# The state's read of an attention and bilinear kernel on 64-row tiles, with its two halves summed after scaling

## The chip, the cores and the metric

The kernel runs on one core of a Trainium2 chip. The metric is the device time of one execution in microseconds (us), lower is better. The core has TensorE (PE in the rows; its weight loads are listed apart as PEld), VectorE (DVE), ScalarE (ACT), GpSimd (POOL) and SyncE (SP), which here only starts transfers. TensorE writes its results into PSUM, which the kernel takes in pairs of banks of 128 partitions by 512 fp32 columns; VectorE and ScalarE read them there and write into SBUF.

## The reference

Each of 8 batches with 8 heads has 512 tokens `x` and 32 states `state`, both 64 wide. Tokens read the states and states read the tokens; all the rows then pass a bilinear layer.

```python
scores = scale * x @ state.T           # per batch and head; a = softmax(scores)
xread = a @ state                      # 512 rows
scores2 = scale * state @ x.T          # a2 = softmax(scores2)
sread = a2 @ x                         # 32 rows: the state's read
rows = concat([xread, sread])          # heads side by side: 4608 x 512 in all
out = ((rows @ w1) * (rows @ w2)) @ w3 @ w_out
```

All inputs and the output are fp32.

## The kernel before

The two last weights are multiplied into one ahead of the batches (`f`, `m` and `k` steps), while `w1` and `w2` come in and are converted. Everything large is computed as a high and a low part: a value is rounded to fp32r (`high`, on ScalarE), the remainder is taken (`low`, on VectorE), and TensorE adds three products of the parts. The state's read and the scores are small and use plain fp32 products; TensorE runs each of these as two passes, so 32 products are 64 records in the trace.

The work is cut into some 1,300 named steps. No scheduler orders them: the tables OPENING, SCRIPTS and CLOSING list their names, and each engine runs its part of the steps in that order. In SCRIPTS, which is followed once for each of batches 2 to 7, `+` stands for the next batch and `*` for the one after it. A batch `b` takes these steps:

- `sP`: scores of states against tokens. 8 products (`per_head`, line 201), each 64 rows deep (one head) and 32 columns of the array wide: two heads times four column strips, hence eight tiles of 64*32, in two PSUM banks, one for each half of the rows. `sM`, `sN`, `sE`, `sA`, `sB` make softmax over tokens with the sum's reciprocal in `sum2`, `sT` to `sV` the softmax over states; `sW` and `sQ` turn the first and move it, so that tokens lie on the partitions (`a2`).
- `u0p` to `u3p`: states against `w1` and `w2`, four steps of 8 products in the same form as `sP` (line 201 too). `u..h` (ScalarE) and `u..l` (VectorE, line 174) split them and so free their banks.
- `rP`: the state's read, line 362. For each of 2 head halves (`kt`), 4 token tiles (`t`) and 4 head pairs (`j`) one product over 128 tokens: 32 columns of the array, 64 moving columns. The four head pairs lie on four column strips of the array (128*32), and the four token tiles are added up in one PSUM bank. `rS` multiplies by the reciprocal of the sum on VectorE (line 371), `rV` transposes (line 378), `rQ` moves 16 blocks into `sread`, which is used at the very end only.
- `a0` to `a7` (line 417): the bilinear factors, 12 products each; `c` copies one factor, `m` multiplies by the other.
- `P1` to `P7` (lines 220 and 225): one level of Strassen products with the fused weight; `v` steps (line 177 and copies) add them up, `d` steps store.

PSUM is handed out as four pairs of banks in rotation from batch 1's `a` steps on: a step on TensorE that starts a new pair takes the one that the fourth such step before it used, and so waits until VectorE and ScalarE have read that one. In the batches 3 to 7 the order on TensorE is `P4`, `u0p`, `rP`, `u1p`, `u2p`, `u3p`, `sP` (of the next batch; batch 7 has none to follow), `P6`, `P7`. So `u1p` takes the pair of `P2` and `P4`, which the last two `v5` sums free; `u3p` takes the pair of `u0p`, which `u0l` frees; `sP` takes the pair of `rP`, which `rS` frees.

Of the kernel before, what the change touches and what calls it, by code (L numbers as in the profile page):

```python
# [57 lines left out]
1:sh g2A 0:o1 g2C 1:sl g2B 1:t 1:u0l 0:d0 g2D 1:sW 0:z2 g30 g2h g2l g3A 1:sQ g31 g3C g3B 0:d1 0:o3 1:u1h 0:o2  # L58
g3D 1:u2h 0:d3 0:rQ 1:u1l 1:u2l g3h g3l 0:d2 paired 1:a0 1:c0 1:u3p 1:m0 1:u3h 2:sP 1:a1 1:rP 1:c1 2:sT 1:u3l
1:a4 2:sM 2:sR 2:sN 2:t 2:sS 1:m1 2:sE 2:sX 2:sC 1:B0d 1:a2 1:A0h 1:c4 1:a3 2:sD 2:sF 2:sG 1:rS 1:a5 1:B0h 1:m4  # L60
2:sV 1:c2 1:a6 1:A0l 1:B0l 2:sW 1:c5 1:c3 1:m2 2:sA 1:m3 1:c6 1:B1d 1:B1h 1:m5 1:A1h 1:a7 1:D0x 1:c7 1:m6 1:A1l
1:B1l 1:m7 1:D1x 1:P1 1:D0y 1:P2 1:E0h 2:sh 2:sl 1:C0h 1:v1a 1:F0h 1:v1b 1:C1h 1:C0l 1:C1l 1:D1y 1:rV 1:v2a
1:E0l 2:sQ 1:P3 1:D1z 3:x 1:G0h 1:F0l 1:F1h 1:E1h 1:v3a 1:F1l 1:v2b 1:P5 1:E1l 1:P4 1:D0z 1:v3b 1:G0l 1:rQ 2:rP
1:G1h 1:v5a 1:G1l 1:H0h 1:v5b 1:v5c 1:H1h 2:u0p 1:v5d 2:sB 1:H0l 2:u1p 2:u2p 2:rS 2:u0h 2:u0l 3:t 2:u1h 2:u2h
2:u1l 3:sP 2:u2l 3:sT 1:d5 2:u3p 2:u3h 3:sM 3:sN 1:P6 1:H1l 1:v6a 3:sE 2:rV 2:u3l 1:d3 1:P7 1:v6b 1:v6c 1:v7a
1:v7b 1:d6 1:d7 2:rQ
# [15 lines left out]
CLOSING = """
7:a0 7:a1 7:a3 7:c1 7:c0 7:m0 7:a2 7:c2 7:m1 7:a5 Rw00h 7:c3 7:m2 7:m3 7:c5 7:A0h 7:a4 7:c4 7:B0d 7:m4 7:m5 7:a6
7:A1h 7:B0h 7:B1d 7:B1h 7:B0l 7:B1l 7:c6 7:a7 7:C0h 7:c7 7:A0l 7:A1l 7:m7 7:m6 Rw01h 7:P1 Rw10h 7:v1a 7:E0h
7:C1h 7:P2 7:E1h 7:D0x 7:D0y 7:v2a 7:C0l 7:v1b 7:D1x 7:F0h 7:C1l 7:D1y 7:v2b 7:D1z 7:F0l 7:F1h R0 7:F1l 7:P3
7:G0h 7:E1l 7:P5 Rw11h 7:v3a 7:D0z 7:G1h 7:E0l 7:v3b 7:G0l 7:P4 7:v5a 7:H0h 7:v5b 7:G1l Rw00l 7:v5c 7:H0l Rw01l
7:v5d 7:P6 7:v6a Ra00 7:d3 Rw10l Ra01 7:H1h 7:v6b 7:v6c Rw20h 7:d5 Rc0 7:H1l Rm0 Rx0 Rw20l Rw11l Ra10 Rw21h
Rw30h 7:P7 Rw30l Ra11 7:d6 Rw31h Rd0 7:v7a Rw21l Ra20 Rw31l Rc1 Ra21 Ra30 Rw40h Rw41h Rc2 RA0h Rw40l Rm1 Rx1
Rw50h Ra31 7:v7b Rw51h Rw41l Rd1 Rw50l Ra40 Ra41 Rm2 RA1h Ra50 Rc3 Rw51l Rm3 Rw60h RA1l Ra51 Rx2 Rw61h Rc4 Rx3
Rw60l Ra60 Rm4 Rw70h Rw61l Rd2 Rd3 Rx4 7:d7 Rc5 RA0l Re0 RA2h Rm5 Rw70l R2P0 Rf0 Rx5 Ra61 Re1 Rg0 R1P0 Rf1 RA3h  # L90
Ra70 R2P1 Rc6 RA3l RF0h RA2l Rw71h RE1h Rm6 Rg1 R2P2 RE0h R2P3 Rv2 Rx6 Rw71l Re2 RE1l R1P1 Rf2 RF0l Rg2 Ra71
RE0l RE2h R1P2 R1P3 RE2l R6P0 Rc7 R4P0 Rm7 R4P1 R6P1 Rx7 R5P0 Re3 R4P2 Rv1 Rf3 R5P1 RE3h R6P2 R5P2 Rg3 RF2h RE3l
R5P3 RF1h RF2l RF3h R4P3 RF1l R6P3 RF3l Rv5 Rv4 R7P0 R7P1 Rv6 Rv8 R7P2 R7P3 R3P0 Rv7 R3P1 R3P2 Ro1 R3P3 Rv3 Ro0
"""


# [955 lines left out]
```

## Time and profile before

| | |
|---|---|
| Median of 3 runs | 480.27 us (480.11 to 480.42) |
| The profiled execution | 480.09 us |
| Its span, first to last instruction | 478.3 us |
| TensorE busy | 472.1 us (99%), 3226 records |
| VectorE busy | 415.0 us (87%), 642 instructions |
| ScalarE busy | 240.0 us (50%) |
| Granted TensorE clock, mean | 0.999 |
| One batch of the loop | 47.24 us |

The span is the profiled execution's, and the execution took 1.8 us more than it. A busy share says what an engine does over the whole; what limits a stretch is told by the waits and by the chain of waits, which goes back from the last instruction to whatever released it, or to the instruction before it on its engine.

### The profile page before, as it was taken

Reading aid. Unit: us, or ns where it says so; the run is one execution under the profiler, and the core shown is the slowest. Engines: PE = TensorE matmul, PEld = TensorE weight load, DVE = VectorE, ACT = ScalarE, POOL = GpSimd, SP = SyncE. Lnnn points to the kernel's source line nnn. Section 1 sums busy time; section 2 is a strip of 40 time slices with the busy share of each in tenths; the row PEclk is TensorE's granted clock in tenths of the full one; section 3 lists DMA queues with packets and bytes.
Section 4 is the critical chain, followed back from the end, with each engine's and each line's share of the span. In section 5 each row is a group of like instructions: output and inputs, shape, how many; then the busy total and the mean of one; then the engine's idle time right before and its main releaser. Section 6 shows DMA issues by size and latency. Waiting matters only on the chain.

```text
span 478.3 us, 8331 instructions
## 1 busy us (share of the span) xinstructions
PE 472.1 (99%) x3226; PEld 364.2 (76%) x3226; DVE 415.0 (87%) x642; ACT 240.0 (50%) x381; POOL 0.2 (0%) x4
## 2 busy tenths in 40 slices
PE   8999999999999999999999999999999999999996
...
DVE  5889998998999988997999799979997996399995
...
GB/s 339 428 423 391 240 165 98 88 112 103 14 121 110 136 105 69 38 121 134 25 43 126 129 31 44 122 126 29 50 124 27 32 37 72 2 0 45 23 24 44
DMA packets 56359, 52.45 MB, mean 110 GB/s; under 512 B 42752, under 2 KB 50944, under 8 KB 51712
## 3 DMA queue, kind: packets, MB, share of 16 engines
...
q8 instruction: 25, 0.41, 0.4%
...
## 4 chain that ended last, share of the span: by engine, by line
PE 92%; DMA 3%; ACT 2%; DVE 1%; issue 0%; SPq 0%; ACTq 0%
PE ps L417 37%; PE ps L220 19%; PE ps L225 10%; PE ps L201 8%; PE ps_o L773 5%; PE ps_o L559 5%; PE ps L847 3%; DMA x_d<-in_x_d_dram 2%; PE ps L362 2%; PE ps L849 2%; DMA raw<-in_w_k_dram 1%; PE ps L951 1%; ACT w_sb L671 1%; PE ps_o L951 1%; ACT ulps L684 1%; DVE w_sb L696 0%
## 5 line engine op out<-in xcount | busy, mean ns | idle before, releaser
L417 PE MATMUL ps<-at_lo,sw_hi 128*128 128x512 f32 x256 | 100.0, 391 | 0.0
L417 PE MATMUL ps<-at_hi,sw_hi 128*128 128x512 f32 x256 | 99.8, 390 | 0.0
L417 PE MATMUL ps<-at_hi,sw_lo 128*128 128x512 f32 x256 | 99.7, 390 | 0.0
L427 ACT COPY tmp<-ps 128x512 f32<-128x512 f32 x64 | 36.1, 586 | 70.6 <-PE ps L417 36.0
L177 DVE TENSOR_TENSOR tmp<-tmp,ps 128x512 f32<-128x512 f32 x81 | 54.6, 681 | 4.6 <-PE ps L225 2.9
L417 PEld LDWEIGHTS ps<-at_lo,sw_hi 128*128 128x128 f32 x256 | 48.1, 188 | 11.6 <-issue 1.7
L220 PE MATMUL ps<-t,g_hi 128*128 128x512 f32 x224 | 56.7, 395 | 0.0
L417 PEld LDWEIGHTS ps<-at_hi,sw_lo 128*128 128x128 f32 x256 | 48.0, 188 | 10.1
L417 PEld LDWEIGHTS ps<-at_hi,sw_hi 128*128 128x128 f32 x256 | 48.1, 188 | 9.8
L220 PEld LDWEIGHTS ps<-t,g_hi 128*128 128x128 f32 x224 | 40.1, 188 | 12.3 <-DVE sw_lo L174 4.3
L180 ACT CAST sw_hi<-ps 128x1024 fp32r<-128x1024 f32 (+1 forms) x34 | 31.4, 970 | 33.1 <-PE ps L201 33.1
L220 PE MATMUL ps<-wo,g_hi 128*128 128x512 f32 x168 | 42.4, 394 | 0.0
L174 DVE TENSOR_TENSOR sw_lo<-ps,sw_hi 128x1024 fp32r<-128x1024 f32 (+1 forms) x34 | 38.0, 1152 | 5.0 <-ACT sw_hi L180 4.6
L446 DVE TENSOR_TENSOR g_x<-tmp,ps 128x512 f32<-128x512 f32 x28 | 18.5, 676 | 22.5 <-ACT tmp L427 22.5
L220 PEld LDWEIGHTS ps<-wo,g_hi 128*128 128x128 f32 x168 | 30.7, 188 | 6.1
L225 PEld LDWEIGHTS ps<-t,g_lo 128*128 128x128 f32 x224 | 30.5, 190 | 2.3
L201 PE MATMUL ps<-w_sb,st 64*32 64x512 f32 (+1 forms) x544 | 31.4, 570 | 0.0
L225 PE MATMUL ps<-t,g_lo 128*128 128x256 f32 x224 | 31.1, 281 | 0.0
L174 DVE TENSOR_TENSOR g_lo<-g_x,g_hi 128x512 fp32r<-128x512 f32 (+2 forms) x50 | 31.1, 630 | 0.0
L180 ACT CAST g_hi<-g_x 128x512 fp32r<-128x512 f32 (+2 forms) x50 | 27.9, 579 | 4.2 <-DVE g_x L446 4.2
L180 ACT CAST g_hi<-raw 128x512 fp32r<-128x512 f32 x42 | 25.3, 620 | 9.4 <-DVE raw L174 6.2
L174 DVE TENSOR_TENSOR g_lo<-raw,g_hi 128x512 fp32r<-128x512 f32 x42 | 28.2, 682 | 0.0
...
## 6 DMA issues: line engine op xcount, KB each, us to landing
...
sread<-turned SPq DMA_DIRECT2D x128, 4.0 KB, 1.8
```

The lines of the kernel that those rows point to most:

```text
L174: nc.vector.tensor_tensor(out=out, in0=x, in1=y, op=ALU.subtract)
L177: nc.vector.tensor_tensor(out=out, in0=x, in1=y, op=ALU.add)
L180: nc.scalar.copy(out=hi, in_=src)
L201: nc.tensor.matmul(ps[j * NS:(j + 1) * NS, q], states[rows, j], moving(rows, j), start=True, stop=True)
L220: nc.tensor.matmul(ps[:, tt].rearrange("p (n d) -> p n d", n=2), g, w(k), start=(fresh and k == 0), stop=False, skip_group_check=True,)
L225: nc.tensor.matmul(ps[:, tt, :HO], g, w(k)[:, 0], start=False, stop=(k == QF - 1), skip_group_check=True)
L417: nc.tensor.matmul(ps[:, i], w[:, kt, c:c + P], a[:, kt], start=(k == 0), stop=(k == 3 * KT - 1))
L427: nc.scalar.copy(out=copies[ft], in_=sums[ft][:, 0])
L446: nc.vector.tensor_tensor(out=whole, in0=copies[ft], in1=sums[ft][:, 1], op=ALU.mult)
L559: nc.tensor.matmul(ps[:, :DO], g, wo[w][:, ft, :], start=(ft == 0 and k == 0), stop=(ft == FT - 1 and k == 2))
L773: nc.tensor.matmul(w34_ps[i][:, :DO], a, w, start=(len(started) == 1 and n == 0), stop=(len(started) == FT and n == len(terms) - 1),)
L847: nc.tensor.matmul(ps[:, i], wh[:, kt], sr[:, kt], start=(kt == 0), stop=False)
```

## The change

Each product of the state's read is cut in two along the tokens: tokens 0 to 63 of a tile on the upper 64 rows of the array, 64 to 127 on the lower 64. There are 64 products instead of 32, on eight tiles of 64*32, and the halves go into the two banks of the pair, each of which is added up over the four token tiles. `rS` scales both banks at once, 256 columns instead of 128. `rV` first adds the two halves, 128 columns within SBUF, and then transposes as before.

```diff
-            ps = two_banks()[:, 0, :KT * D].rearrange("p (k d) -> p k d", k=KT)
+            ps = two_banks()[:, :, :KT * D].rearrange("p i (k d) -> p i k d", k=KT)
             for kt in range(KT):
                 for t in range(NT):
                     for j in range(NP):
                         mine = slice(j * NS, (j + 1) * NS)
-                        nc.tensor.matmul(
-                            ps[mine, kt], s["a2"][:, kt, t * P + j * NS:t * P + (j + 1) * NS],
-                            s["tokens"][:, t, 2 * j + kt], start=(t == 0), stop=(t == NT - 1),
-                        )
+                        for i in range(2):
+                            rows = slice(i * D, (i + 1) * D)
+                            nc.tensor.matmul(
+                                ps[mine, i, kt], s["a2"][rows, kt, t * P + j * NS:t * P + (j + 1) * NS],
+                                s["tokens"][rows, t, 2 * j + kt], start=(t == 0), stop=(t == NT - 1),
+                            )
...
-            s["scaled"] = att.tile([P, KT, D], F32, name="scaled", bufs=1)
+            s["scaled"] = att.tile([P, 2, KT, D], F32, name="scaled", bufs=1)
             nc.vector.tensor_tensor(
-                out=s["scaled"], in0=s["read"], in1=s["sum2"].unsqueeze(2).broadcast_to([P, KT, D]), op=ALU.mult
+                out=s["scaled"], in0=s["read"], op=ALU.mult,
+                in1=s["sum2"].unsqueeze(1).unsqueeze(3).broadcast_to([P, 2, KT, D]),
             )
...
+            both = s["scaled"].rearrange("p i k d -> p i (k d)")
+            add(both[:, 0], both[:, 0], both[:, 1])
             s["turned"] = att.tile([P, KT, D], F32, name="turned")
-            nc.vector.transpose(
-                out=s["turned"].rearrange("p k d -> p (k d)"), in_=s["scaled"].rearrange("p k d -> p (k d)")
-            )
+            nc.vector.transpose(out=s["turned"].rearrange("p k d -> p (k d)"), in_=both[:, 0])
```

The three tables list the same step names in a new order, from batch 1's `sh` on; two lines show the manner.

```diff
-F1h +sl F1l D0z G0h P3 E0h v2b E0l P5 E1h E1l H0h D1z v3a G1h v5a P4 +u0p v3b G1l v5b H1h +rP G0l v5c d3 v5d
-+u0h *t +u1p +u2p +u1h +u2h +rS +u0l +u3p *sP H0l +u1l +u2l +u3h +u3l +rV *sM P6 v6a H1l P7 *sN *sT v6b v6c +rQ
...
+P5 v2a E1l E0l v3a v2b G0h D0z P4 v3b v5a +u0p D1z H0h v5b G0l v5c H1h v5d +rP +u1p G1h G1l +u0h +u1h +u0l +rS
+d3 +u1l +u2p +u2h +u3p +u3h H0l *sP P6 H1l +u2l *sM *sN v6a *t d5 +u3l P7 *sT +rV ?x v6b v6c *sR +rQ *sE v7a v7b
```

On TensorE most of the order stays. In each batch `a1` now comes ahead of `a0` and `a4` ahead of `a3`; batch 1 takes its `a` steps as 2, 3, 5, 4, 7, 6 instead of 4, 2, 3, 5, 6, 7; batch 2's read moves behind its `u0p`; and a few products of the closing change places with each other. At three places the order of the instructions before and after reads as follows. In such a row stand the line, the operation, what is written from what, the output's partitions and columns, and how many such instructions follow each other.

TensorE in batch 4, from the end of `P4` on (L220, L225) over `u0p`, `rP`, `u1p` to `u3p` and `sP` to `P6`; before:

```order
L225 MATMUL ps_2355<-t,g_lo 128x256 x8
L201 MATMUL ps_2471<-w_sb,st 32x512 x8
L362 MATMUL ps_2484<-x_s,e_2375 32x64 x32
L201 MATMUL ps_2527<-w_sb,st 32x512 x8
L201 MATMUL ps_2536<-w_sb,st 32x512 x8
L201 MATMUL ps_2554<-w_sb,st 32x512 x8
L201 MATMUL ps_2563<-x_d,st 32x512 x8
L220 MATMUL ps_2583<-t,g_hi 128x512 x8
```

And now:

```order
L225 MATMUL ps_2497<-t,g_lo 128x256 x8
L201 MATMUL ps_2597<-w_sb,st 32x512 x8
L364 MATMUL ps_2617<-x_s,e_2480 32x64 x64
L201 MATMUL ps_2682<-w_sb,st 32x512 x8
L201 MATMUL ps_2705<-w_sb,st 32x512 x8
L201 MATMUL ps_2717<-w_sb,st 32x512 x8
L201 MATMUL ps_2730<-x_d,st 32x512 x8
L220 MATMUL ps_2739<-t,g_hi 128x512 x8
```

The places are the same; the read is 64 products instead of 32.

VectorE at the same place, from the `v5` sums (L177) over the read's scaling (L371, now L373) and the subtractions `u0l` to `u3l` (`sw_lo`) to the transpose of the read (L378, now L383); `g_lo` are splits for the products `P6` and `P7`. Before:

```order
L177 TENSOR_TENSOR tmp<-tmp,ps_2355 128x512 x2
L371 TENSOR_TENSOR scaled<-ps_2484,sum_2137 128x128
L174 TENSOR_TENSOR sw_lo<-ps_2471,sw_hi 128x1024
L174 TENSOR_TENSOR g_lo<-raw,g_hi 128x512
L174 TENSOR_TENSOR sw_lo<-ps_2527,sw_hi 128x1024
L174 TENSOR_TENSOR sw_lo<-ps_2536,sw_hi 128x1024
L174 TENSOR_TENSOR sw_lo<-ps_2554,sw_hi 128x1024
L378 STREAM_TRANSPOSE turned<-scaled 128x128
```

And now:

```order
L177 TENSOR_TENSOR tmp<-tmp,ps_2497 128x512 x2
L174 TENSOR_TENSOR g_lo<-g_x,g_hi 128x512
L174 TENSOR_TENSOR sw_lo<-ps_2597,sw_hi 128x1024
L373 TENSOR_TENSOR scaled<-ps_2617,sum_2275 128x256
L174 TENSOR_TENSOR sw_lo<-ps_2682,sw_hi 128x1024
L174 TENSOR_TENSOR g_lo<-raw,g_hi 128x512 x2
L174 TENSOR_TENSOR sw_lo<-ps_2705,sw_hi 128x1024
L266 TENSOR_REDUCE m_2758<-ps_2730 128x2
L270 TENSOR_SCALAR m_2758<-m_2758 128x2
L177 TENSOR_TENSOR tmp<-tmp,ps_2739 128x512
L174 TENSOR_TENSOR sw_lo<-ps_2717,sw_hi 128x1024
L276 STREAM_TRANSPOSE work<-ps_2730 128x1024
```

The scaling has moved behind `u0l`, one split ahead of `u0l`, and the last two subtractions go later; the new sum and the transpose follow the last of these rows.

TensorE in batch 2, from the end of `P4` to `P6`; before:

```order
L225 MATMUL ps_1309<-t,g_lo 128x256 x8
L362 MATMUL ps_1453<-x_s,e_1351 32x64 x32
L201 MATMUL ps_1497<-w_sb,st 32x512 x8
L201 MATMUL ps_1509<-w_sb,st 32x512 x8
L201 MATMUL ps_1518<-w_sb,st 32x512 x8
L201 MATMUL ps_1542<-x_d,st 32x512 x8
L201 MATMUL ps_1556<-w_sb,st 32x512 x8
L220 MATMUL ps_1571<-t,g_hi 128x512 x8
```

And now:

```order
L225 MATMUL ps_1401<-t,g_lo 128x256 x8
L201 MATMUL ps_1530<-w_sb,st 32x512 x8
L364 MATMUL ps_1539<-x_s,e_1363 32x64 x64
L201 MATMUL ps_1608<-w_sb,st 32x512 x8
L201 MATMUL ps_1618<-w_sb,st 32x512 x8
L201 MATMUL ps_1629<-w_sb,st 32x512 x8
L201 MATMUL ps_1641<-x_d,st 32x512 x8
L220 MATMUL ps_1673<-t,g_hi 128x512 x8
```

The read has gone from the head of the run to its second place, as in the later batches.

## Rows read from the trace of the kernel before

**Rows 1.** The page's busy times, share of the span and instructions of each engine, and the slices of TensorE and VectorE: busy tenths in 40 equal slices of the span.

```profile
PE 472.1 (99%) x3226; PEld 364.2 (76%) x3226; DVE 415.0 (87%) x642; ACT 240.0 (50%) x381; POOL 0.2 (0%) x4
...
PE   8999999999999999999999999999999999999996
...
DVE  5889998998999988997999799979997996399995
```

**Rows 2.** TensorE's waits over the whole span, all that there are: who waited for whom, us in total, times, longest us.

```profile
PE ps_o L738 <- DVE w_sb L696: 1.2, 1, 1.2
PE ps_o L143 <- DVE work L140: 1.0, 1, 1.0
PE ps L201 <- DMA x_d<-in_x_d_dram: 0.2, 1, 0.2
```

**Rows 3.** The chain of waits in order of time, TensorE's pieces of line L201 that stand between others with no read of the state ahead of them (the last one has it ahead): start, us, what, records.

```profile
72.98 1.88 PE ps L201 x32
...
83.24 1.02 PE ps L201 x16
...
100.73 2.74 PE ps L201 x48
```

**Rows 4.** The same chain at the eight reads of the state (L362), batches 0 to 7, with the pieces of L201 beside them; for batch 2 from the chain of the stretch 153 to 160 us.

```profile
99.70 1.03 PE ps L362 x64
...
122.41 1.03 PE ps L362 x64
...
153.97 1.03 PE ps L362 x64
155.00 4.54 PE ps L201 x80
159.54 0.04 issue
...
201.23 1.02 PE ps L201 x16
202.25 1.05 PE ps L362 x64
203.30 3.59 PE ps L201 x64
...
248.48 1.02 PE ps L201 x16
249.50 1.03 PE ps L362 x64
250.53 3.59 PE ps L201 x64
...
390.19 1.02 PE ps L201 x16
391.21 1.03 PE ps L362 x64
392.24 2.73 PE ps L201 x48
```

**Rows 5.** The instructions of line L362 in batches 1 to 7: duration min/median/max in ns, first and last start, form (rows*columns of the array, then the moving operand).

```profile
L362 PEld LDWEIGHTS ps<-x_s,e x448: 106/110/110, 122.3 to 392.0; 128*32 128x32 f32 x150
L362 PE MATMUL ps<-x_s,e x448: 216/219/243, 122.3 to 392.0; 128*32 128x64 f32 x150
```

**Rows 6.** VectorE's groups of instructions by line and form: out<-in, count, busy us, mean ns of one, idle before and what ended it. A sum out of PSUM, the read's scaling, and a sum of 128 columns within SBUF.

```profile
L177 DVE TENSOR_TENSOR tmp<-tmp,ps 128x512 f32<-128x512 f32 x81 | 54.6, 681 | 4.6 <-PE ps L225 2.9 <-ACT tmp L859 0.3
...
L371 DVE TENSOR_TENSOR scaled<-ps,sum 128x128 f32<-128x128 f32 x8 | 2.3, 289 | 3.5 <-PE ps L362 3.5
...
L177 DVE TENSOR_TENSOR tmp<-g_x,tmp 128x128 f32<-128x128 f32 x4 | 1.1, 288 | 0.1
```

**Rows 7.** One batch of the loop, from one `u0p` to the next: the stretch and its length, then busy us (records) of PE, PEld, DVE, ACT and POOL, granted clock, DMA share, GB/s.

```profile
248.41:295.65 47.24, 47.24 (x353) 37.38 (x352) 42.25 (x63) 21.05 (x35) 0.00 (x0) 1.00 0.28 82
```

**Rows 8.** VectorE's timeline at batch 5's read: start, us, engine, line, operation, count, idle before it and what ended that.

```profile
295.98 1.40 DVE L177 TENSOR_TENSOR tmp<-tmp,ps 128x512 f32<-128x512 f32 x2
297.84 0.29 DVE L371 TENSOR_TENSOR scaled<-ps,sum 128x128 f32<-128x128 f32 x1 [0.47 <-PE ps L362]
298.05 1.21 DVE L174 TENSOR_TENSOR sw_lo<-ps,sw_hi 128x1024 fp32r<-128x1024 f32 x1
299.18 0.68 DVE L174 TENSOR_TENSOR g_lo<-raw,g_hi 128x512 fp32r<-128x512 f32 x1
```

**Rows 9.** TensorE's timeline at the same place.

```profile
295.65 1.09 PE L201 MATMUL ps<-w_sb,st 64*32 64x512 f32 x16
296.67 1.10 PE L362 MATMUL ps<-x_s,e 128*32 128x64 f32 x64
297.70 2.81 PE L201 MATMUL ps<-w_sb,st 64*32 64x512 f32 x48
300.30 1.06 PE L201 MATMUL ps<-x_d,st 64*32 64x512 f32 x16
301.30 0.50 PE L220 MATMUL ps<-t,g_hi 128*128 128x512 f32 x1
```

**Rows 10.** The page's DMA queues that carry instructions: packets, MB, share of 16 engines' span.

```profile
q8 instruction: 25, 0.41, 0.4%
```

**Rows 11.** The first tenth of a microsecond of batch 5's `u1p`, line L201 alone: the stretch and its length, busy us (records) of PE and of PEld, granted clock, DMA share, GB/s.

```profile
297.68:297.78 0.10, 0.08 (x8) 0.08 (x16) 1.00 0.00 0
```

More of the change, by code (lines that the diff above doesn't have):

```diff
@@ L57 @@
 0:l7 1:sF 0:e7 g1B 1:sA 0:rP g1D 1:u0p g1C 1:sB g1h 1:sG 0:rS 0:o0 1:u1p g1l 1:u2p g20 0:z3 1:sV 0:rV g21 1:u0h
[L58 to L66, printed above, removed]
+1:sh g2A 0:o1 g2C 1:sl g2B 1:t 1:sW 1:sQ 1:u0l 0:d0 g2D 0:z2 g30 g2h g2l g3A g31 g3C g3B 0:d1 0:o3 1:u1h 0:o2
+g3D 1:u2h 0:d3 0:rQ 1:u1l 1:u2l g3h g3l 0:d2 paired 1:a0 1:u3p 2:sP 1:c0 1:m0 2:sM 1:u3h 1:a1 1:c1 1:u3l 2:sT
+2:sN 3:x 1:rP 2:sR 2:sE 2:sS 2:sX 2:sA 1:rS 1:m1 1:B0d 1:a2 1:a3 1:a5 2:sC 1:c2 1:B0h 1:m2 2:sD 2:sF 1:c3 1:B0l
+2:sG 1:m3 1:c5 1:rV 1:a4 1:A0h 2:sV 1:c4 1:B1d 1:a7 2:sW 1:A0l 1:B1h 1:A1h 1:a6 1:c7 1:m4 1:m5 1:D0x 1:m7 1:B1l
+1:C0h 1:C0l 2:sB 1:c6 1:A1l 1:m6 1:D1x 1:D0y 2:t 2:sQ 1:P1 1:P2 1:v1a 1:C1h 1:F0h 1:v1b 1:C1l 1:E0h 1:P3 1:D1y
+1:E1h 1:G0h 1:D1z 1:E1l 1:F1h 1:D0z 1:F0l 1:F1l 1:P5 1:v3a 1:E0l 1:v2a 1:v3b 1:v2b 2:sh 2:sl 1:H0h 1:G0l 1:v5a
+1:v5b 1:P4 1:v5c 1:rQ 1:v5d 1:H0l 2:u0p 2:rP 1:G1h 2:u0h 2:u1p 2:u0l 2:u3p 2:rS 2:u2p 2:u1h 3:sP 2:u3h 2:u1l
+2:u2h 2:u3l 1:G1l 3:sT 3:sM 1:H1h 4:x 1:d3 2:u2l 3:sN 1:H1l 1:P6 1:v6a 1:v6b 2:rV 2:a1 3:sR 3:sE 1:v6c 1:P7 2:c1
+1:d5 2:a0 1:d6 1:v7a 1:v7b 2:c0 1:d7 3:t 2:a2 2:rQ
 """
@@ L70 @@
     None: """
-+sA a0 +sR a1 c0 c1 m0 m1 *x B0d +sS A0h A0l B0h B0l a2 +sX a3 +sC +sD +sF +sG c2 m2 c3 +sV a4 m3 c4 m4 B1d B1h
-A1h a5 c5 +sB a6 +sW m5 c6 B1l m6 C0h C0l A1l a7 D0x +sh c7 m7 P1 v1a D0y D1x F0h P2 v1b C1h D1y +sQ F0l C1l v2a
-F1h +sl F1l D0z G0h P3 E0h v2b E0l P5 E1h E1l H0h D1z v3a G1h v5a P4 +u0p v3b G1l v5b H1h +rP G0l v5c d3 v5d
-+u0h *t +u1p +u2p +u1h +u2h +rS +u0l +u3p *sP H0l +u1l +u2l +u3h +u3l +rV *sM P6 v6a H1l P7 *sN *sT v6b v6c +rQ
-d5 *sE d6 v7a v7b d7
++sS m0 m1 +sA A0h B0d A0l B0h +sX a4 a3 +sC +sD +sF +sG c3 c2 B0l +sB m2 m3 +sV a5 c4 B1d m4 c5 B1h A1h a6 m5
+D0x a7 c6 m6 c7 C0h +sW +sh A1l D0y C0l B1l m7 P1 +sQ P2 D1x F0h D1y v1a C1h v1b +sl E0h C1l E1h P3 F0l F1h F1l
+P5 v2a E1l E0l v3a v2b G0h D0z P4 v3b v5a +u0p D1z H0h v5b G0l v5c H1h v5d +rP +u1p G1h G1l +u0h +u1h +u0l +rS
+d3 +u1l +u2p +u2h +u3p +u3h H0l *sP P6 H1l +u2l *sM *sN v6a *t d5 +u3l P7 *sT +rV ?x v6b v6c *sR +rQ *sE v7a v7b
+d6 +a1 +a0 +a2 +c0 d7 +c1
 """,
@@ L82 @@
 CLOSING = """
[L83 to L92, printed above, removed]
@@ L93 @@
-R5P3 RF1h RF2l RF3h R4P3 RF1l R6P3 RF3l Rv5 Rv4 R7P0 R7P1 Rv6 Rv8 R7P2 R7P3 R3P0 Rv7 R3P1 R3P2 Ro1 R3P3 Rv3 Ro0
+7:m0 7:a3 7:c2 7:m1 7:a4 7:m2 7:B0d 7:a5 7:c3 7:c5 7:m3 7:c4 7:B0h 7:B0l 7:A1h Rw00h 7:A0h 7:a6 7:m4 7:m5 7:c6
+7:a7 7:B1d 7:D0x 7:A0l 7:C0h 7:m6 7:A1l 7:c7 7:m7 7:B1h 7:B1l 7:P1 7:E0h 7:C1h Rw01h 7:C0l 7:D0y 7:v1a 7:P2
+7:C1l 7:v1b 7:F0h 7:E1h 7:P3 7:D1x 7:D1y 7:E1l 7:F0l 7:D0z 7:F1h 7:v2a 7:E0l 7:F1l 7:v3a 7:G0h 7:v3b 7:v2b 7:D1z
+7:d3 Rw00l 7:P5 R0 7:v5a 7:P4 7:G0l 7:H0h 7:G1h 7:v5b 7:G1l 7:P6 7:H1h 7:v5c 7:v5d Ra00 7:H0l 7:v6a Rw10h Rw11h
```

7 lines of the change are left out of this document (added).

## The prediction

> **What bounds the kernel now.** I read the busy times first, then TensorE's waits, then the chain of waits, then the two neighbourhoods that the change touches. TensorE is busy for 472.1 of 478.3 us, with a 9 in 38 of the 40 slices, and VectorE for 87% [rows 1]. TensorE's own list of waits holds 2.4 us in all, and all of it comes before the pieces that the new order touches: the three names in it are the zeros of the warm-up, a weight conversion and the first load of x [rows 2]. So from about 35 us on the time is what TensorE's instructions take one behind the other. A change can gain only by making that sequence shorter, and it can lose by making TensorE wait. No order of the same instructions can win more than those 2.4 us, and the new order leaves that stretch alone; so I credit the reordering with no gain.
>
> The sequence is read best from the chain of waits, because its pieces run from start to start. A step of eight products on 64*32 tiles (line L201, 16 records, two passes for each fp32 product) takes 1.02 us when it stands alone, two in a row take 1.88, three 2.74 [rows 3], four 3.59 [rows 4]. So one more step of this form costs 0.86, and about 0.16 is paid once for each unbroken run, at its ends. Eight products lie on eight tiles (two halves of rows, four of columns), so a step is two passes deep: 0.43 us for 512 columns, 0.84 ns for a column. The state's read (L362) is 64 records of 64 columns on 128*32 tiles [rows 5]; on four tiles that is 16 passes deep, 16 x 64 x 0.84 ns = 0.86 us. The chain gives it 1.03 [rows 4]. The 0.17 beyond the passes is again the price of the ends. In six of the eight batches the read stands beside steps of the other form: first in such a run in batches 0 and 2, inside it in 3 to 7, so there the run of 64*32 steps is cut and its 0.16 is paid twice.
>
> **The read itself.** It becomes 128 records on 64*32 tiles. They lie on eight tiles instead of four, so they stay 16 passes deep: 0.86 us again, and no gain inside. What goes are the ends. I take 0.88 for a read in the middle of a run, 0.02 for the doubled starts. The floor is 0.86, since the same 64 columns go through each tile 16 times and the 64-row form has no faster column in any row; the upper end of this term is 1.03, if the read still pays its own ends. That the pairs may not run side by side at all is the first rival.
>
> Batches 3 to 6, from the step before the read to the end of the run [rows 4]: 1.02 + 1.05 + 3.59 = 5.66 once and 1.02 + 1.03 + 3.59 = 5.64 three times; after: 1.02 + 4 x 0.86 + 0.88 = 5.34. That is 0.32 + 3 x 0.30 = 1.22. Batch 7 has one step less: 1.02 + 1.03 + 2.73 = 4.78 against 4.48, 0.30. Batch 0: 1.03 [rows 4] + 2.74 [rows 3] = 3.77 against 1.02 + 2 x 0.86 + 0.88 = 3.62, 0.15. Batch 2 now takes 1.03 + 4.54 + 0.04 of issue = 5.61 [rows 4]; its five steps alone would be 4.46, so 0.12 of it is waiting for VectorE, which I leave in: 4.46 + 0.88 + 0.12 = 5.46, 0.15 (0.27 if the waiting goes). Batch 1's read stands between 128*128 products and stays alone: 0.88 + 0.16 = 1.04 against 1.03, a loss of 0.01. Sum: 1.22 + 0.30 + 0.15 + 0.15 - 0.01 = 1.81 us less.
>
> **VectorE's additions.** The scaling reads 256 columns instead of 128. From 289 ns for 128 columns and 681 for a 512-column sum out of PSUM [rows 6] a column costs 1.02 ns, so 0.13 more. The new sum over 128 columns is the form that takes 288 ns in the same list. That is 0.42 us a batch: 42.25 of 47.24 us [rows 7] becomes 42.67 of about 46.9. The cover is the 4 us that VectorE stays idle; without it each batch would be 0.42 longer, 3.4 in all. ScalarE, at half its time, gets nothing. The transpose and the copies behind it only have to land before the last rows are read.
>
> **Waits at the seam.** With the run shorter, TensorE asks earlier for two banks. The step after the read takes the bank that two sums (L177 x2) free at 295.98 + 1.40 = 297.38 [rows 8]; it started at 297.70 [rows 9]. It would now start 0.86 + 0.88 and some part of 0.16 behind 295.65, at 297.39 to 297.55. The third step after the read takes the bank of the step that stands ahead of the read, freed by the subtraction at 298.05 + 1.21 = 299.26; it started at 297.70 + 0.88 + 0.86 = 299.44. It would now ask at 299.11 to 299.27. In the new order this subtraction no longer stands behind the scaling, which had waited 0.47 us for the read; one split of 0.68 us goes ahead of it instead, so it runs about 297.90 to 299.11. A bank is passed on in about 0.04 (the issue piece in [rows 4]). Both margins shrink to between 0.12 and nothing: I take 0.02 a batch for six batches, 0.1, with ends of 0 and 0.15 a batch (0.9). The scaling itself now ends at about 299.5, ahead of the next scores, which take its bank at about 300.0. The first 128*128 product after the run takes the bank of the first step after the read, and the subtraction that frees this bank moves up by one split, so that margin grows. In the batches' other places the new order swaps neighbours (second product step before the first, fifth before the fourth). No row prices that; the nearest is the 0.12 of waiting in batch 2. I take 0, with ends of 0 and 0.5 over the kernel; below nothing is excluded by [rows 2].
>
> **Instructions fetched.** The queue with 25 packets and 0.41 MB [rows 10] carries, by its count, TensorE's 6,452 records: 258 to a packet, 0.4% x 16 x 478.3 / 25 = 1.2 us each. One read now is 256 records, a packet's worth, in 0.9 us. If a read begins just where a packet does, TensorE may wait for the next: 0 to 1.2 us in a batch, likely in none or one. I take 0 and keep 1.2 for the range.
>
> Sum: 1.81 - 0.1 = 1.7 less. The profiled execution took 480.09 us for its span of 478.3; that gives 478.4. Against the median of 480.27 it is 478.6. I forecast 478.5.
>
> **Rivals.** *The instructions come too slowly* (slower). One read issues 256 records (128 products' passes and as many weight loads) in the time of 128. The densest long stretch of the trace is the present read, 128 records in 1.03 us, 8.0 ns each. At that pace a read takes 2.06, less ends 1.9, which is 1.0 more in each of eight: 478.5 + 8 = 486.5. It decides from 0.88 + 1.7/8 = 1.09 us a read, 4.3 ns a record. For it: nothing in the trace has been faster for so long. Against it: the 1.03 is already explained by columns and ends, and at the head of a run 8 matmuls and 16 weight loads start within 0.08 us, 3.3 ns each [rows 11], on the very tiles that the read will use. The Trainium skill, "TensorE: Matmul & The Clock Gate", section "Wait — 56ns, not 53.3ns?", says that start-to-start never drops below about 25 ns however small a matmul is; by it 128 starts would be an estimated 3.2 us a read, over 17 us more in all. This trace does not agree: 64 starts in 1.03 us are 16 ns each.
>
> *The ends stay* (no effect). If a run is broken by any new operand and not by the tile's form, the read pays its ends as before: no gain, 480.2. Against it: the scores, from other tensors than the three steps ahead of them, join their run: the piece of 3.59 in [rows 4] holds them, 0.85 above three steps; in [rows 9] they follow without a gap.
>
> *The gain is waited away* (within 0.2%). At 0.15 a batch in six batches, 0.5 in swapped places and no other loss, 478.4 + 1.3 = 479.7.
>
> **How the numbers follow.** A difference of 0.2%, 0.96 us, is about what a measurement of this kernel can tell from none. The forecast, 477.8 to 479.3, has 0.62. Waited away has 0.12, ends stay 0.07, together the 0.19 of no change; slow supply, in full or in part (481.2 to 486.5), has 0.17; 0.02 lies below. So faster 0.64, same 0.19, slower 0.17. The range goes from 477.6 to 481.3 and leaves out the slow supply.
>
> **What would show it.** In the chain after, a run of the batches 3 to 6 with the read inside is one stretch of about 5.34 us, and the read adds 0.88 to it; a read near 1.9 is the first rival, 1.03 with 0.16 on either side the second. The third step after the read shows no idle time, or some hundredths behind the subtraction. The scaling takes 0.42 and the new sum 0.29. The period of a batch falls from 47.24 to about 46.95. I am wrong if TensorE's list of waits holds more than 1 us beyond the 2.4 of now.

## The result, and the profile after

The changed kernel takes 486.6 us (median of 4 runs, 486.52 to 487.71) against 480.25 (480.11 to 480.42) on the same chip: 1.0137 times as long, 95% interval 1.012 to 1.0155. It is slower by 6.35 us; the forecast was 1.7 faster. The profiled execution has a span of 484.8 us, 6.5 more than before, at the same granted clock (1.0).

The page's busy times after, and its queue of TensorE's instructions (packets, MB, share of 16 engines), against [rows 1, 10]:

```profile
PE 476.0 (98%) x3738; PEld 371.1 (77%) x3738; DVE 421.5 (87%) x650; ACT 241.2 (50%) x381; POOL 0.2 (0%) x4
...
q8 instruction: 29, 0.48, 0.4%
```

TensorE's waits after, against [rows 2]: who waited for whom, us, times, longest us.

```profile
PE ps_o L741 <- DVE w_sb L699: 2.0, 1, 2.0
PE ps L201 <- issue: 1.7, 2, 1.2
```

TensorE is busy for 3.9 us more and waits for 2.7 more in its whole list, above the 1 us at which I had said that I would be wrong. The entry of 1.7 us is new and names no engine: in two places a step of line L201 waited for nothing that the profile shows. The chain of waits at the reads of batches 1, 3, 4 and 7, against [rows 4] (start, us, what, records):

```profile
123.32 1.50 PE ps L364 x91
...
205.35 1.77 PE ps L201 x32
207.68 1.95 PE ps L201 x32
...
251.21 1.02 PE ps L201 x16
252.23 1.39 PE ps L364 x92
253.62 3.48 PE ps L201 x64
257.10 2.04 PE ps L220 x8
...
397.40 1.17 issue
398.57 2.80 PE ps L201 x44
```

Even where it stands alone, in batch 1, the read takes 1.50 instead of 1.03 us. In batch 4, from the step ahead of the read to the first 128*128 product, the run is 257.10 - 251.21 = 5.89 instead of 5.64. Batch 3 has a hole ahead of 207.68, batch 7 one of 1.17 ahead of 398.57. The chain puts the border between step and read where the pipeline empties; from the starts of the instructions, which I use from here on, the runs are these (us, batches 0 to 7):

| | 0 | 1 | 2 | 3 | 4 | 5 | 6 | 7 | sum |
|---|---|---|---|---|---|---|---|---|---|
| before | 3.77 | 1.03 | 5.68 | 5.66 | 5.64 | 5.64 | 5.65 | 4.79 | 37.86 |
| forecast | 3.62 | 1.04 | 5.46 | 5.34 | 5.34 | 5.34 | 5.34 | 4.48 | 35.96 |
| after | 4.58 | 1.50 | 6.04 | 6.62 | 5.89 | 5.96 | 6.32 | 7.22 | 44.13 |

They hold 6.27 of the span's 6.5 us. Two things are in them. First, the reads go slowly in all batches. The instructions of line L364 alone, in stretches that all begin with the read (batch 1, then batch 4): the stretch and its length, busy us and records begun so far of PE and of PEld, clock, DMA share, GB/s.

```profile
123.25:123.52 0.27, 0.27 (x33) 0.27 (x33) 1.00 0.11 15
123.25:123.66 0.41, 0.41 (x39) 0.41 (x43) 1.00 0.08 10
123.25:124.06 0.81, 0.81 (x82) 0.81 (x86) 1.00 0.08 10
123.25:124.60 1.35, 1.35 (x127) 1.34 (x128) 1.00 0.06 8
...
252.02:252.27 0.25, 0.25 (x16) 0.25 (x12) 1.00 0.00 0
252.02:252.46 0.44, 0.44 (x38) 0.44 (x39) 1.00 0.00 0
252.02:253.40 1.38, 1.38 (x127) 1.38 (x123) 1.00 0.00 0
```

The same of the read before, in batch 4:

```profile
249.43:249.65 0.22, 0.22 (x16) 0.22 (x20) 1.00 0.20 74
249.43:249.87 0.44, 0.44 (x32) 0.44 (x36) 1.00 0.62 221
249.43:250.31 0.88, 0.88 (x63) 0.88 (x64) 1.00 0.43 149
```

Before, 16 passes start in each 0.22 us: the columns' pace, evenly. After, in batch 1, 33 start in the first 0.27, about the pace that the columns allow on eight tiles (55 ns for eight); then almost none for 0.14; then 43 in 0.40 and 45 in 0.54. As many weight loads start in that first 0.27, so the loads by themselves can go at the faster pace. Start by start, eight take 67 ns behind the first break (16 records, 4.2 ns each), and every third or fourth eight 95 to 150. In batch 4 there is an earlier break as well: only 16 in the first 0.25.

Second, some steps behind reads wait long. TensorE's timeline in batch 7 (start, us, line, form, count, idle before it):

```profile
394.07 1.09 PE L201 MATMUL ps<-w_sb,st 64*32 64x512 f32 x16
394.96 1.59 PE L364 MATMUL ps<-x_s,e 64*32 64x64 f32 x128
396.35 1.05 PE L201 MATMUL ps<-w_sb,st 64*32 64x512 f32 x4
398.57 2.80 PE L201 MATMUL ps<-w_sb,st 64*32 64x512 f32 x44 [1.17 <-issue]
```

Transfers between 396.0 and 398.6 us: busy tenths in 40 slices of 65 ns (a packet is entered in the slice in which it starts), and the only queue that moved anything.

```profile
DMA  0900000000000000000000000000000000000000
...
q8 instruction: 1, 0.02, 2.7%
```

`u1p` stops after 4 of its 16 records. One packet of 16 KB with TensorE's instructions starts at 396.10, and the step goes on at 398.57, 2.47 us later. The hole in batch 3 is alike: packet 205.15, on at 207.68.

VectorE after, by line and form, against [rows 6]: the scaling, now of 256 columns, and the new sum.

```profile
L373 DVE TENSOR_TENSOR scaled<-ps,sum 128x256 f32<-128x256 f32 x8 | 3.3, 416 | 1.5 <-PE ps L364 1.5
...
L177 DVE TENSOR_TENSOR scaled<-scaled 128x128 f32<-128x128 f32 x8 | 2.1, 262 | 0.0
```

### The profile page after: what moved, and what is told of

It reads as the page before. It is cut to its first block, busy times and chain, and to the rows that moved or that the text cites. A ratio compares the mean times of both kernels' runs of the same rounds, so it can differ in the third digit from the quotient of the medians.

```text
span 484.8 us, 9354 instructions
## 1 busy us (share of the span) xinstructions
PE 476.0 (98%) x3738; PEld 371.1 (77%) x3738; DVE 421.5 (87%) x650; ACT 241.2 (50%) x381; POOL 0.2 (0%) x4
## 4 chain that ended last, share of the span: by engine, by line
PE 92%; DMA 3%; ACT 2%; issue 1%; DVE 1%; SPq 0%; ACTq 0%
PE ps L420 36%; PE ps L220 19%; PE ps L225 10%; PE ps L201 8%; PE ps_o L776 5%; PE ps_o L562 5%; PE ps L850 3%; PE ps L364 2%; DMA x_d<-in_x_d_dram 2%; PE ps L852 2%; DMA raw<-in_w_k_dram 1%; PE ps L954 1%; ACT w_sb L674 1%; PE ps_o L954 1%; ACT ulps L687 1%
## 5 line engine op out<-in xcount | busy, mean ns | idle before, releaser
L177 DVE TENSOR_TENSOR tmp<-tmp,ps 128x512 f32<-128x512 f32 x81 | 55.1, 682 | 5.3 <-PE ps L225 3.0
L220 PE MATMUL ps<-t,g_hi 128*128 128x512 f32 x224 | 56.7, 395 | 0.0
L220 PEld LDWEIGHTS ps<-t,g_hi 128*128 128x128 f32 x224 | 40.1, 188 | 12.2 <-DVE sw_lo L174 3.4
L174 DVE TENSOR_TENSOR sw_lo<-ps,sw_hi 128x1024 fp32r<-128x1024 f32 (+1 forms) x34 | 39.1, 1157 | 10.5 <-ACT sw_hi L180 9.8
L220 PE MATMUL ps<-wo,g_hi 128*128 128x512 f32 x168 | 42.4, 394 | 0.0
L201 PE MATMUL ps<-w_sb,st 64*32 64x512 f32 (+1 forms) x544 | 33.8, 570 | 1.7 <-issue 1.7
L220 PEld LDWEIGHTS ps<-wo,g_hi 128*128 128x128 f32 x168 | 30.7, 188 | 6.2
L225 PEld LDWEIGHTS ps<-t,g_lo 128*128 128x128 f32 x224 | 30.5, 190 | 2.3
L225 PE MATMUL ps<-t,g_lo 128*128 128x256 f32 x224 | 31.2, 282 | 0.0
```

Of the source, the lines that this page charges most:

```text
L174: nc.vector.tensor_tensor(out=out, in0=x, in1=y, op=ALU.subtract)
L201: nc.tensor.matmul(ps[j * NS:(j + 1) * NS, q], states[rows, j], moving(rows, j), start=True, stop=True)
L220: nc.tensor.matmul(ps[:, tt].rearrange("p (n d) -> p n d", n=2), g, w(k), start=(fresh and k == 0), stop=False, skip_group_check=True,)
L225: nc.tensor.matmul(ps[:, tt, :HO], g, w(k)[:, 0], start=False, stop=(k == QF - 1), skip_group_check=True)
```

## The experiments

The expectations use three names. S: TensorE gets its records too slowly for the new read. C: the two row halves conflict, each pair of products being served in part one after the other. O: the new order costs the time. The control is the kernel before on the same chip, 480.13 to 480.26 us in all of them. `order_only`, `read_only`, `spread` and `quarters` were executed 4 to 10 times, the others once, and each left one trace. Executions of after differ by up to 1.2 us, so of the others I read the trace and not a small difference in the total. Later the long holes got a theory of their own: the fetch of instructions.

**The order alone, the read alone.** `order_only` has the new order and the old read; `read_only` the new read and the old order.

```diff
 order_only, against after
-            ps = two_banks()[:, :, :KT * D].rearrange("p i (k d) -> p i k d", k=KT)
+            ps = two_banks()[:, 0, :KT * D].rearrange("p (k d) -> p k d", k=KT)
...
 read_only, against after (its three tables are those of before)
-P5 v2a E1l E0l v3a v2b G0h D0z P4 v3b v5a +u0p D1z H0h v5b G0l v5c H1h v5d +rP +u1p G1h G1l +u0h +u1h +u0l +rS
+F1h +sl F1l D0z G0h P3 E0h v2b E0l P5 E1h E1l H0h D1z v3a G1h v5a P4 +u0p v3b G1l v5b H1h +rP G0l v5c d3 v5d
```

> The read of before (32 products on 128*32 tiles) in the new order. Theory S (the read's 256 records use up TensorE's instructions faster than they come): nothing but the order is left, so 480.2 plus or minus 0.5, reads of 1.03 us each, no wait named issue. Theory C (the two halves of rows disturb each other): the same. Theory O (the new order costs): 485 to 487. This run parts O from the other two.

> The read on 64-row halves with its scaling and sum, in the order of before. S and C: reads of 1.35 to 1.55 us as after, 484 to 488; under S some of the waits named issue fall on other batches, since the records ahead of them are the same in number but the places within a packet depend on the order. O: 478 to 481.

`order_only` takes 480.47 us, 1.0005 of before (0.9996 to 1.0014); `read_only` 486.54, 1.0128 (1.0113 to 1.0144). O falls: the whole loss is the read's. TensorE's timeline of `order_only` in batch 4 has the read of before, 1.03 from its start to the next step's:

```profile
248.58 1.09 PE L201 MATMUL ps<-w_sb,st 64*32 64x512 f32 x16
249.60 1.10 PE L362 MATMUL ps<-x_s,e 128*32 128x64 f32 x64
250.63 2.81 PE L201 MATMUL ps<-w_sb,st 64*32 64x512 f32 x48
```

**Many records without halves.** `thin` is the kernel before, with its order, its 128*32 tiles and its one bank, and cuts each product of the read by its moving columns, 2 x 32: 256 records in the read, as after, and the columns of before.

```diff
 thin, against before
-                        nc.tensor.matmul(
-                            ps[mine, kt], s["a2"][:, kt, t * P + j * NS:t * P + (j + 1) * NS],
-                            s["tokens"][:, t, 2 * j + kt], start=(t == 0), stop=(t == NT - 1),
-                        )
+                        for i in range(2):
+                            cols = slice(i * NS, (i + 1) * NS)
+                            nc.tensor.matmul(
+                                ps[mine, kt, cols], s["a2"][:, kt, t * P + j * NS:t * P + (j + 1) * NS],
+                                s["tokens"][:, t, 2 * j + kt, cols], start=(t == 0 and i == 0),
+                                stop=(t == NT - 1), skip_group_check=True,
+                            )
```

> The kernel of before, all 128 rows in each product, but each product cut into two of 32 moving columns: 64 products, 256 records a read as in the changed kernel, with no halves of rows and one bank. S: reads of 1.35 to 1.6 us in place of 1.03, the first 64 records at the pace of the columns and the rest slower, and waits named issue in some batches: 483 to 488. C: reads of about 1.03 us, 480 to 481. (A weight load that no longer hides behind half as many columns would lengthen the reads evenly from the first record on.)

487.29 us. TensorE's timeline in batch 4:

```profile
252.14 1.48 PE L364 MATMUL ps<-x_s,e 128*32 128x32 f32 x128
253.55 2.81 PE L201 MATMUL ps<-w_sb,st 64*32 64x512 f32 x48
```

The read takes 1.41, as after, though no halves run side by side, and a long hole comes in batch 7 here too (2.14 us). Halves are not needed for the loss. In all of its reads but batch 1's (which breaks off after 8 passes and takes 1.86) the first 32 passes start within 0.30 us, somewhat slower than the columns' 0.22, the next break comes there, and then eight take 67 ns.

**Many columns for the same records.** `wide` lets each product of after move 128 columns, both heads of a pair (the half that is not wanted is computed and dropped; two scalings instead of one). The records stay 256, the passes need 1.72 us.

```diff
 wide, against after
...
-                                ps[mine, i, kt], s["a2"][rows, kt, t * P + j * NS:t * P + (j + 1) * NS],
-                                s["tokens"][rows, t, 2 * j + kt], start=(t == 0), stop=(t == NT - 1),
+                                ps[mine, i, kt, :2], s["a2"][rows, kt, t * P + j * NS:t * P + (j + 1) * NS],
+                                s["tokens"][rows, t, 2 * j:2 * j + 2], start=(t == 0), stop=(t == NT - 1),
...
```

> The changed kernel with 128 moving columns in each product of the read (both heads of a pair, of which the scaling takes the one that is meant, in two instructions): the same 256 records, twice the columns. S: each eight matmuls now need about 110 ns of columns, more than the 67 to 80 ns in which their records come, so the reads take 1.75 to 1.8 us at an even pace and the waits named issue are gone or small: 485 to 487. C: the halves disturb each other column by column, so the reads take twice what they take now, 2.7 to 3.1 us, 495 or more.

489.03 us, outside what I expected, since the holes of batches 3 and 7 stayed. TensorE's timeline in batch 4:

```profile
253.21 2.08 PE L364 MATMUL ps<-x_s,e 64*32 64x128 f32 x127
255.04 0.65 PE L201 MATMUL ps<-w_sb,st 64*32 64x512 f32 x6
```

Its read alone, in stretches that all begin with it (columns as above):

```profile
253.21:253.65 0.44, 0.44 (x27) 0.44 (x30) 1.00 0.00 0
253.21:254.09 0.88, 0.88 (x59) 0.88 (x58) 1.00 0.00 0
253.21:254.97 1.76, 1.76 (x123) 1.76 (x122) 1.00 0.00 0
```

In the runs the read takes 1.75 to 1.84 where 1.72 is the columns' floor (1.96 in batch 1, where it stands alone), and behind the first 0.4 us eight passes start every 109 ns without a break, 6.8 ns a record. So eight tiles do work side by side on the two row halves, and C falls; behind its head a read of the same 256 records is not held up when each has twice the time.

**Fewer records at once.** `half` takes two of the four token tiles; `spread` puts the read in three pieces (24, 24 and 16 products) behind `u0p`, `u1p` and the next step.

```diff
 half, against after
-                for t in range(NT):
+                for t in range(NT // 2):
...
 spread, against after
-P5 v2a E1l E0l v3a v2b G0h D0z P4 v3b v5a +u0p D1z H0h v5b G0l v5c H1h v5d +rP +u1p G1h G1l +u0h +u1h +u0l +rS
-d3 +u1l +u2p +u2h +u3p +u3h H0l *sP P6 H1l +u2l *sM *sN v6a *t d5 +u3l P7 *sT +rV ?x v6b v6c *sR +rQ *sE v7a v7b
+P5 v2a E1l E0l v3a v2b G0h D0z P4 v3b v5a +u0p D1z H0h v5b G0l v5c H1h v5d +rPa +u1p +rPb G1h G1l +u0h +u1h +u0l +u2p +rPc +rS
+d3 +u1l +u2h +u3p +u3h H0l *sP P6 H1l +u2l *sM *sN v6a *t d5 +u3l P7 *sT +rV ?x v6b v6c *sR +rQ *sE v7a v7b
...
```

> The changed kernel with only the first two of the four token tiles in the read, so half of the state's read is left out: 32 products, 128 records, on the same eight tiles. Columns alone would take 0.43 us inside a run. S: the first 64 records at that pace, the rest a little slower, 0.43 to 0.55, the waits named issue mostly gone, 475 to 477.5 in all. C: half of what the read takes now, 0.68 to 0.78 us, 477.5 to 480.

> The changed kernel with the read cut into three pieces of 24, 24 and 16 products, which stand behind the first, second and third of the 64*32 steps (batch 0 in two pieces, batch 1 in one as it stood). The number of records, tiles and banks is the same. S: the steps between the pieces need only 32 records in 0.86 us, so TensorE's store of instructions fills up again; most of the 6.3 us come back and part of the forecast gain with it, 478.3 to 481, and the waits named issue shrink or go. C: the pieces take as long together as the whole, 485 to 488. O: unchanged, 486 to 487.

`half` takes 478.16 us, `spread` 486.77 (1.0132, 1.0116 to 1.0149). Both missed. TensorE in `half`, batch 4:

```profile
247.29 1.09 PE L201 MATMUL ps<-w_sb,st 64*32 64x512 f32 x16
248.18 0.97 PE L364 MATMUL ps<-x_s,e 64*32 64x64 f32 x64
248.96 2.95 PE L201 MATMUL ps<-w_sb,st 64*32 64x512 f32 x48
```

VectorE at the same place:

```profile
247.40 1.41 DVE L177 TENSOR_TENSOR tmp<-tmp,ps 128x512 f32<-128x512 f32 x2 [0.30 <-PE ps L225]
...
249.54 1.23 DVE L174 TENSOR_TENSOR sw_lo<-ps,sw_hi 128x1024 fp32r<-128x1024 f32 x1
```

The read takes 0.78 in the run. Its passes start over 0.75 us, with the breaks of after's first half, but the sums that free `u1p`'s bank also end at 247.40 + 1.41 = 248.81, 0.15 ahead of `u1p`'s start at 248.96. So 0.78 is a floor that VectorE sets as well. The breaks are not VectorE's: in batch 1, where the read stands alone, its 64 passes also start over 0.64 us, where the columns need 0.43. In `spread` the first piece takes the same 0.78: in batch 5 41 of its 48 passes have started by 0.45, the sums end at 300.96 and `u1p` starts at 301.11. About 0.25 of `spread`'s loss in each run is this wait, which the read of before covered. Its next two pieces take 0.49 and 0.36 instead of the columns' 0.32 and 0.22: shorter pieces still have breaks, single eights of up to 0.16 us. The runs come to 6.19 where no hole is in them (and holes came too: batches 3 and 6 took 7.08 and 7.16).

**What the holes hang on.** `shift` and `shift64` issue 32 and 16 products of one column behind the warm-up, 128 and 64 records more at the start of the kernel, and nothing else (`range(16)` in `shift64`).

```diff
+    for n in range(32):
+        mine = slice(n % 4 * 32, n % 4 * 32 + 32)
+        nc.tensor.matmul(unused[mine, :1], zeros[:, mine], zeros[:, :1], start=True, stop=True)
```

> The changed kernel with 32 products of one column behind the warm-up (128 records, half of a packet of instructions), in a time in which TensorE waits for the first weights. S, in the part on packets: the reads keep 1.35 to 1.55 us, but the waits named issue and the long pieces of L201 behind the reads move from batches 0, 3, 6 and 7 to others, and their sum changes from the 4 to 5 us of now. If these waits have another cause, they stay in the same batches with the same lengths. C and O say nothing of it.

> As the run with 128 more records behind the warm-up, with 64. If the waits named issue come from where a packet of instructions ends, they fall on another set of batches again, neither 0, 3, 6, 7 nor 2, 5, and each ends about 2.5 us behind the start of a packet; the reads themselves stay at 1.35 to 1.6 us. If not, they stand where they stood in the changed kernel.

| runs, us | 0 | 1 | 2 | 3 | 4 | 5 | 6 | 7 |
|---|---|---|---|---|---|---|---|---|
| after | 4.58 | 1.50 | 6.04 | 6.62 | 5.89 | 5.96 | 6.32 | 7.22 |
| `shift` (487.24 us) | 4.05 | 1.51 | 8.31 | 5.82 | 5.89 | 7.47 | 5.88 | 5.02 |
| `shift64` (488.08 us) | 4.05 | 1.53 | 6.96 | 7.88 | 5.88 | 5.88 | 8.33 | 5.19 |

With 128 records more at the start, the holes of batches 0, 3, 6 and 7 are gone and come in 2 and 5; with 64 more they stand in 2, 3 and 6, in batch 3 at another place (at the end of the read). TensorE's timeline in `shift`, batch 2 (its lines stand three further down):

```profile
156.49 1.82 PE L367 MATMUL ps<-x_s,e 64*32 64x64 f32 x128
158.11 1.06 PE L204 MATMUL ps<-w_sb,st 64*32 64x512 f32 x7
160.35 2.35 PE L204 MATMUL ps<-w_sb,st 64*32 64x512 f32 x37 [1.18 <-issue]
```

Its packet starts at 157.72, 2.63 ahead of 160.35; in batch 5 302.70 and 305.15. So the holes belong to places in the stream of instructions, not to batches. That they only fall differently in each execution is unlikely: `read_only`, `thin`, `wide` and `early`, which have no records more at the start, all have holes in batches 3 and 7, where `shift` has none. `shift64` met my wording only in part, as 3 and 6 recur.

**The waits at the head.** In batch 4 after, `u0p` starts at 251.14 and the read at 252.02. The instructions of line L364 there (ns min/median/max, first and last start) include nine waits on semaphores in TensorE's queue:

```profile
L364 PEldq EVENT_SEMAPHORE  x9: 51/51/51, 251.2 to 252.2; - x9
```

Before, the same nine:

```profile
L362 PEldq EVENT_SEMAPHORE  x9: 51/51/51, 248.4 to 249.3; - x9
```

Each lasts 51 ns, and they start 0.11 to 0.13 us apart; most of them stand for the 16 moves of `a2`. Before, the last was over at 249.39, ahead of the read at 249.43; after, the read begins 0.88 behind the step ahead instead of 1.02, and runs into the last ones, at 252.03 and 252.16: there lies its early break. `early` lets one product of one column ahead of `u0p` take over these waits.

```diff
+                if n == 0 and b > 1:
+                    nc.tensor.matmul(ps[:, 0, :1], s["a2"][:, 0, :P], s["tokens"][:, 0, 0, :1], start=True, stop=True)
```

> The changed kernel with one product of a single column ahead of the first 64*32 step in batches 2 to 7, whose weights are the first 128 columns of the moved softmax. It takes over the waits for the 16 moves, 8 semaphores in all, which in the changed kernel stand before the first eight products of the read. If these waits keep TensorE's store of instructions empty at the head of the reads inside a run, those reads now start as the ones of batches 0 and 1 do (32 matmuls within 0.27 us) and take 1.25 to 1.3 us in place of 1.35 to 1.55; time 485 to 486.5, waits named issue aside. If the waits are harmless, the reads stay at 1.35 to 1.55 us, and the time rises by the 0.1 us of each new product, 487.

486.43 us. TensorE's timeline in batch 4:

```profile
252.03 1.52 PE L364 MATMUL ps<-x_s,e 64*32 64x64 f32 x128
253.35 2.82 PE L201 MATMUL ps<-w_sb,st 64*32 64x512 f32 x48
```

The read takes 1.32 instead of 1.42. The reads of batches 4 to 7 gain 0.08 to 0.15 each, less than I expected. A break at the head stays: in batch 4 the first 16 passes go at full pace, the next eight take 0.17 us and each eight behind them 66 to 85 ns. So the waits are a part of the early break and not all of it. The rest of the read's cost stays, as do holes in batches 3, 6 and 7.

**Small pieces.** `small` has three pieces of 8 products each in batches 2 to 7; `quarters` four pieces of 16 (the whole read) with the product of `early`, and `u1p`'s pair of banks handed out ahead of the read's.

```diff
 small, against after (order as in spread)
+            for kt, t in ([(0, 0), (0, 1), (1, 0)] if b > 1 else [divmod(n, NT) for n in range(2 * NT)])[first:last]:
...
 quarters, against after (+rPa +u1p +rPb .. +u2p +rPc +u2h +u3p +rPd +rS)
+            if first == 0 and b > 1:
+                s["ahead"] = two_banks()
...
+                ps = units[n] = s["ahead"] if n == 1 and b > 1 else two_banks()
```

> The kernel with the read in pieces, with 8 products in each of the three pieces of batches 2 to 7 (five eighths of those reads are left out; the waits for the moves stay at the first piece). A piece is 32 records. If a store of about 64 records stands ahead of TensorE and only what goes beyond it comes slowly, the second and third piece take their columns' 0.11 us: a run of batches 4 and 5 takes 4.46 + 0.33 + 0.1 to 0.25 for the first piece's waits, 4.9 to 5.05. If each change between the two kinds of step costs something of its own, as the 0.85 us beyond the columns in the pieces of 24 could also be read, the run takes 5.2 or more.

> All of the read, in four pieces of 16 products (64 records) behind the four 64*32 steps of a batch, with the waits taken over by one early product as in the other run. With a store of 64 records, less some 16 to 24 that the step ahead still holds, each piece has 40 to 48 records at the columns' pace and the rest slower: 0.25 to 0.35 us a piece, a run of 5.5 to 5.8 us against 5.89 to 6.0 in the changed kernel and 5.64 before, and with shorter waits named issue 481 to 485. If the pieces' price is the change between the steps, 6.3 us a run and 487 or more.

`small` takes 482.13 us with runs of 5.72, `quarters` 488.97 (1.0177, 1.016 to 1.0194) with runs of 6.59 and more. Both missed. TensorE's timeline of `small` in batch 4:

```profile
249.95 1.09 PE L201 MATMUL ps<-w_sb,st 64*32 64x512 f32 x16
250.84 0.54 PE L364 MATMUL ps<-x_s,e 64*32 64x64 f32 x16
251.62 1.09 PE L201 MATMUL ps<-w_sb,st 64*32 64x512 f32 x16 [0.24 <-DVE tmp L177]
```

And of `quarters`:

```profile
252.53 1.09 PE L201 MATMUL ps<-w_sb,st 64*32 64x512 f32 x16
254.08 0.45 PE L367 MATMUL ps<-x_s,e 64*32 64x64 f32 x31 [0.46 <-DVE tmp L177]
```

In `small` the first piece with what follows takes 0.78 instead of 0.11, and `u1p` waits for the same sums: again the floor, 0.88 + 0.78 = 1.66 behind `u0p`'s start. From `u1p`'s start to the end of the run it is 4.05, where four steps (3.59) and two pieces of 0.11 make 3.81: each later piece of 32 records costs 0.12 more than its columns, so a price for the change between the two kinds of step is not excluded. In `quarters` the pair that these sums free went to the read, so the read waits there: 0.67 of each run is a wait that my edit made. But behind that wait, with TensorE idle for 0.46, the first 32 passes start in 0.24 us, the full pace of the columns; the later pieces of the same size, which follow a step at once, take 0.42, 0.34 and 0.34. Here a burst of 64 records ran at full pace when TensorE had stood still ahead of it.

## Why the prediction was wrong

**What failed** is the step "The read itself": 0.88 us, because 128 products' passes on eight tiles are 16 deep. The depth was right (`wide` reaches its columns' floor), but a read of 256 records is not bound by its columns. From its start to the next step's it takes 1.35 to 1.55 us in the runs and 1.50 in batch 1. The first rival names this cause, and its 486.5 is the time that came, but that is luck, by another sum: it has 8.0 ns a record in eight reads, and the trace has 4.2 ns between breaks and 1.41 us / 256 = 5.5 ns over batch 4's read. That lies above the break-even of 4.3 ns that the text gives. The argument that I set against this rival was the head of a run, 3.3 ns a record [rows 11]: that is a burst of 24 records, and says nothing about 256.

**The term "Instructions fetched"** was taken as 0 and is the other half. `shift` shows the runs of batches 0, 3, 6 and 7 without a hole (4.05, 5.82, 5.88, 5.02); against them after loses 0.53 + 0.80 + 0.44 + 2.20 = 3.97 us. The sum over the runs is 44.13 - 35.96 = 8.17 above the forecast: 3.97 of holes, and 4.20, or 0.5 a read, of slow reads. "0 to 1.2 us in a batch, likely in none or one" was too small in both: up to 2.2, in four batches. I had priced the packet by the time that its transfer takes (1.12 us here), but TensorE goes on 2.2 to 2.8 us behind its start in the 18 holes of all the runs that I could pair with a packet. Without any hole the runs would sum to 40.16, still 2.3 above before: the change would lose without the packets too. That is a sum from two kernels; none ran so.

**What held.** TensorE's sequence sets the time, and 6.27 of the 6.5 us lost lie in its runs at the reads. The ends do go once: the step ahead of the read takes 0.88 instead of 1.02. But in batch 4 the read's early break gives most of this back: the nine waits at its head, which lay in that time, now reach into the read, and `early`, which takes them away, gains 0.09 of the 0.14. I had not counted them. The order costs nothing (`order_only`), as taken. The scaling takes 416 ns and the sum 262, where 0.42 and 0.29 were said; a batch of VectorE is 43.18 of 47.48 us after, and 42.74 of 47.24 in `order_only`, and TensorE's list names no wait for it in the batches (the row is batch 4, to be read as [rows 7]):

```profile
251.14:298.62 47.48, 47.48 (x418) 38.54 (x417) 43.18 (x63) 21.36 (x35) 0.00 (x0) 1.00 0.28 81
```

**The seams** cost nothing after, since the slow read never reaches them. `half` shows that they were judged well: its third step behind the read starts at 250.82, 0.05 behind the end of the subtraction (249.54 + 1.23 = 250.77), and some 0.14 later than its place. A read of 0.88 would have stood 0.1 above VectorE's floor of 0.78. Only the passing on of a bank, taken as 0.04, took longer behind the sums: 0.15 (0.05 behind the subtraction).

**The rule on small products** that I weighed, 25 ns from start to start, gives 3.2 us a read; no read of after shows it, with 1.35 to 1.55. The Trainium skill gives the right sign there and the wrong size. A line of the same page's opening table, "TensorE: Matmul & The Clock Gate", says that TensorE's queue holds 64; the trace agrees with it in batch 1 after and in `thin`, where about 64 records (32 passes with their weight loads) start first and the break comes behind them; a piece of `quarters` with 64 records had no break at all behind an idle stretch.

**Open.** Why pieces that follow a step at once break after 16 to 24 passes was not settled; that the step ahead still fills part of a store of 64 would fit, and so would a price for each change between the steps; no run parts the two. Nor does a run show what sets the 67 ns for 16 records, or the breaks between them. What makes a packet start, and how much TensorE still holds then, stays open too: packets of after at 158.20, 254.07 and 301.25 us meet the same run and bring no hole. No version here that computes the whole read beats the kernel before.
